# A fused attention, Fourier-mixing and feed-forward kernel: new constants for its list scheduler, and four pieces of work on other engines or queues

## The chip, the cores and the metric

The kernel runs on one core of one Trainium2 chip. The metric is the device time of one execution in microseconds (us). Before the change it is 1061.13 us, the median of three runs (1060.88 to 1061.39).

## What is computed

```python
# attention: q, k, v of 8 batches x 8 heads x 576 positions x 64
mask_plain = (rel >= 0) & (rel < 32)                    # heads 0 to 3
mask_dil   = (rel >= 0) & (rel < 128) & (rel % 4 == 0)  # heads 4 to 7
attn_out = softmax(where(mask, q @ k.T / 8, -1e9)) @ v
x = attn_out, heads side by side                        # (8, 576, 512)
mixed = real(fft(fft(x, axis=1), axis=2))
u  = x + mixed
un = (u - mean(u)) / sqrt(var(u) + 1e-6)                # over the 512 channels
out = u + relu(un @ w_ch1) @ w_ch2                      # 512 -> 2048 -> 512
```

The weights arrive as 64-bit floats, and the kernel turns them into 32-bit ones itself. Products that need full precision are done in three matmuls: each operand is split into a high and a low part (`hi*hi + lo*hi + hi*lo`).

## The kernel before, in words

The kernel is not written in the order in which it runs. A class `Plan` collects operations (`add`: engine, an estimated cost, what is read and written, a priority), and `Plan.run` then plays a list schedule: each engine that is free takes the available operation of lowest priority number whose buffers are free. The order so found is emitted once; on the chip each engine works through its own list in that order and waits on semaphores. Constants at the top of the file (`P_QK`, `P_MIX0`, `P_FILL` and so on) shift the priorities of kinds of work, others say how many buffers or units are treated in one way.

The work has two phases.

In the first phase (0 to 588 us of the trace) there are 96 **attention units**, 12 in each batch, six of dilated heads and six of plain ones; batch 0 begins with the dilated ones. A unit takes two blocks of 96 positions of two heads: eight score matmuls (L582), four masked copies with a running minimum on VectorE (L591), four exponentials on ScalarE (L597), four transposes (L610), a copy (L613), eight matmuls with v (L617), and on VectorE the division by the sums (L625 to L629) into a tile `xt`. Each pair of heads needs three loads, `tq`, `kb` and `vt` (L566 to L568), issued on SyncE's DMA queue (SP). The finished `xt` goes to DRAM from the same queue (`store`, L681). The plain heads of batch 0 go straight into the tiles `x` and `xtail` of the next step (`place`, L646, 11 DMAs).

After a batch's attention comes its **mix** (`mix`): three **folds** add and subtract mirrored rows (t1, t2 at L770 and L772, low parts at L792 and L794), matmuls along the sequence (L821, L843) and along the channels (L867, L873) follow with tables of cosines and sines, then `add_u` on GpSimd (POOL, L734 and L736), and `normalise`. Batch 0's tiles are transposed on TensorE (L715), those of the others come back from DRAM. The two tables are loaded from GpSimd's DMA queue by `tables_after`: `seq` after attention unit number NSEQ, `chn` after unit number NCHN.

Each pair of normalised tiles is a **fill** (`fill`): up-projection (L997) and down-projection (L1013) with the first six of 16 column blocks of the weights. Its weights are 12 tiles of 512 KB, each narrowed from 64 bits by four VectorE operations (L942 to L951) and split (`two_parts`: high part on ScalarE, L957; low part, L959, on POOL or, for the first NLW tiles, on VectorE).

In the second phase (from 588 us) the other ten blocks are applied to chunks of 512 tokens (L1277, L1369, L1336).

The eight PSUM banks are shared out by unit number. The scores of units below NSC2 use two pairs of banks in turn (`half2`), one of which is the pair `mix`; no `mix` bank is given out before the last of these units is done with it. The products with v of units below NAV2 use two banks in turn (`av2`), one of which belongs to `ff`; no fill gets an `ff` bank before the last of these is free. Until the first `ff` bank is given out, the planner puts **filler matmuls** on zeros (L515, two at a time, NSPIN tries) wherever TensorE has nothing else; from then on they vanish.

The change touches the constants, `dma` (L493), `place`, `normalise` and `fold`. What sets the first phase's order beside them are these lines:

```python
tables: if num == NSEQ: add("POOL", 0.3, ... tensor_copy(out=gone(), in_=xt()...))   # L537, L544
plan.behind.update({"av": ("av2",), "ff": ("av2",), "half": ("half2",), "mix": ("half2",)})
add("PE", 0.22, turn_over, (blank,), (spin,), SPIN, at=0.4 * n)                       # L515
```

Of the kernel before, what the change touches and what calls it, by code (L numbers as in the profile page):

```python
# [14 lines left out]
AF = mybir.ActivationFunctionType  # L15
ALU = mybir.AluOpType

B, H, S, D = 8, 8, 576, 64
C, FF = 512, 2048
P = 128  # L20
# [16 lines left out]
NPE = 1  # L37
LO1 = 'DVE'
NFA = 5
NSC2, NAV2 = 21, 32  # L40
NU0, NU1 = 9, 9
NFD, NUD, NLW = 1, 0, 0
P_QK0, P_V0 = -8, -7
P_ST, P_FD, P_WD, P_ST0, P_FD0, P_SPAN0, P_SPAN1 = -9.92, -2.8, -14.79, -21.37, -25.12, 7.59, 23.92
P_QK, P_V, P_TR, P_MIX, P_SPAN, P_W, P_WF, P_FILL, P_FILLT = -7.53, -11.06, -5.0, 3.7, 13.0, 27.01, 3.96, 47.55, 3.61
P_MIX0, P_MIX1 = -24.21, 7.67
NSEQ, NCHN = 4, 10
NCH = B * S // TOK
NREST = 4 * B
QB = 96  # L50
# [135 lines left out]
class Plan:  # L186
# [21 lines left out]
    def add(self, eng, cost, fn, r=(), w=(), prio=0.0, nbytes=0, at=0.0):  # L208
        op = Op()
        op.eng, op.cost, op.fn, op.prio, op.nbytes = eng, cost, fn, prio, nbytes  # L210
        op.num, op.after, op.ready, op.start = len(self.ops), [], at, None
        self.ops.append(op)
        deps, bufs = set(), {}
        for items, writes in ((r, False), (w, True)):
            for it in items:
                b, key = it if isinstance(it, tuple) else (it, None)
                bufs[id(b)] = b
                keys = set(b.writer) | set(b.readers) if key is None else {key, None}
                for x in keys:
                    if x in b.writer:  # L220
                        deps.add(b.writer[x])
                    if writes:
                        deps.update(b.readers.get(x, ()))
        for items, writes in ((r, False), (w, True)):
            for it in items:
                b, key = it if isinstance(it, tuple) else (it, None)
                if writes:
                    if key is None:
                        b.writer, b.readers = {None: op.num}, {}
                    else:  # L230
                        b.writer[key] = op.num
                        b.readers.pop(key, None)
                else:
                    b.readers.setdefault(key, []).append(op.num)
        op.bufs = list(bufs.values())
        for b in op.bufs:
            b.left += 1
        deps.discard(op.num)
        op.waits = len(deps)
        for d in deps:  # L240
            self.ops[d].after.append(op)
        return op
# [119 lines left out]
def act(n):  # L362
    return n * 0.00083 + 0.1
# [27 lines left out]
def fused_kernel(ctx: ExitStack, tc, q, k, v, w1, w2, seq, tail, chn, alt, mask, ident, perm, flip, out):  # L391
    nc = tc.nc
    plan = Plan()
    add = plan.add
# [50 lines left out]
    def work(tag, shape, dtype=F32, bufs=2):  # L445
        return plan.buf(lambda: pools["mix"], tag, shape, dtype, bufs)
# [46 lines left out]
    def dma(fn, r, w, prio, nbytes, slow=1):  # L493
        return add("SP", 0.5, fn, r, w, prio, nbytes * slow)

    def start():
# [139 lines left out]
    def place(u, val, xt, prio):  # L638
        tiles = (xs[0], xs[2], xtail[0]), (xs[1], xs[3], xtail[1])
        for n, (e, row, side, lo, rows) in enumerate((  # L640
# [3 lines left out]
        )[u]):  # L644
            x, p0 = tiles[e][row // P], row % P
            dma(lambda x=x, p0=p0, side=side, lo=lo, rows=rows: nc.sync.dma_start(  # L646
                out=x()[p0:p0 + rows, 0:C // 2], in_=val()[lo:lo + rows, side]),
                (xt,), ((x, ("plain", u, n)),), prio + P_ST0, rows * 1024)

# [42 lines left out]
    def normalise(u, idx, prio):  # L692
        stats, ve, r0, r1 = (work(t, [P, n]) for t, n in (("stats", 6), ("ve", 1), ("r0", 1), ("r1", 1)))
        uc = work("uc", [P, C + 2], F32, NUC)
        add("DVE", 0.6, lambda: nc.vector.bn_stats(out=stats(), in_=u()[:, 0:C]), ((u, 0),), (stats,), prio)
        add("DVE", 0.08, lambda: nc.vector.bn_aggr(out=uc()[:, C:C + 2], in_=stats()), (stats,), ((uc, 1),), prio)
        add("DVE", 0.4, lambda: nc.vector.tensor_scalar(
            uc()[:, 0:C], u()[:, 0:C], uc()[:, C:C + 1], None, op0=ALU.subtract), ((u, 0), (uc, 1)), ((uc, 0),), prio)
        add("DVE", 0.07, lambda: nc.vector.tensor_scalar(
            ve(), uc()[:, C + 1:C + 2], EPS, None, op0=ALU.add), ((uc, 1),), (ve,), prio + 1)  # L700
        add("POOL", 0.47, lambda: nc.gpsimd.tensor_tensor(
            out=r0(), in0=ve(), in1=half(), op=ALU.pow), (ve, half), (r0,), prio + 1)
        add("DVE", 0.07, lambda: nc.vector.tensor_scalar(
            r1(), ve(), r0(), r0(), op0=ALU.mult, op1=ALU.mult), (ve, r0), (r1,), prio + 1)
        add("DVE", 0.07, lambda: nc.vector.tensor_scalar(
            r1(), r1(), -0.5, 1.5, op0=ALU.mult, op1=ALU.add), (r1,), (r1,), prio + 1)
        add("DVE", 0.07, lambda: nc.vector.tensor_scalar(
            uc()[:, C + 1:C + 2], r1(), r0(), None, op0=ALU.mult), (r0, r1), ((uc, 2),), prio + 1)
        dma(lambda: nc.sync.dma_start(out=u_rows(idx), in_=uc()), (uc,), ((us[idx // 4], idx % 4),), prio + 1, P * 2056)
        return uc  # L710
# [28 lines left out]
    def mix(b, when):  # L739
# [10 lines left out]
        def fold(m, prio):  # L750
            early = prio + (P_FD if b else P_FD0)
            n = P if m < 2 else 33
            cs = slice(0 if b else C // 2, C)
            if m < 2:
                xp, xm = tiles[m]
                at = slice(0, P)
                for x, src in ((xp, plus), (xm, minus)):
                    dma(lambda x=x, src=src: nc.sync.dma_start(out=x()[:, cs], in_=src()[P * m:P * m + P, cs]),
                        (src,), ((x, 0),), early, P * (2048 if b else 1024))
            else:  # L760
                xp, xm = xtail
                at = slice(o, o + n)
                for x, key, src, lo, p0, k in (
                    (xp, 0, plus, 256, o, 32), (xm, 0, minus, 256, o, 32),
                    (xp, 1, minus, 288, o + 32, 1), (xm, 1, minus, 0, o + 32, 1),
                ):
                    dma(lambda x=x, src=src, lo=lo, p0=p0, k=k: nc.sync.dma_start(
                        out=x()[p0:p0 + k, cs], in_=src()[lo:lo + k, cs]), (src,), ((x, key),), early, k * 2048)
            t1, t2 = work("t1", [P, NEH], F32, 1), work("t2", [P, NEH], F32, 1)
            either(b < NFD, NEH, lambda on: on.tensor_tensor(  # L770
                out=t1()[at], in0=xp()[at, 0:NEH], in1=xm()[at, C:C // 2 - 1:-1], op=ALU.add), (xp, xm), (t1,), prio)
# [688 lines left out]
```

## Time and profile before

| what | value |
|---|---|
| median of 3 runs | 1061.13 us |
| the profiled execution's own time | 1064.29 us |
| its span, first to last instruction | 1062.5 us |
| TensorE busy | 1053.0 us of the span |
| VectorE, ScalarE, GpSimd busy | 775.7, 516.5, 272.8 us |
| mean granted TensorE clock | 0.998 of full speed |

Busy time is read from the recorded start and end of each instruction; consecutive matmuls overlap, so a stretch in which TensorE is always busy may still hold short waits. PE is TensorE, PEld its weight loads, DVE is VectorE, ACT ScalarE, POOL GpSimd, SP SyncE. A DMA queue's issuing instructions are listed under SPq or POOL.

### The profile page before, as it was taken

To read this page: it belongs to the slowest core of one execution; us is meant where nothing else is said; L and a number is where in the kernel's file an instruction comes from. 1 tells how busy PE (TensorE), PEld (TensorE's weight loads), DVE (VectorE), ACT (ScalarE), POOL (GpSimd) and SP (SyncE) were. 2 spreads that over 40 slices of the span, in tenths; PEclk is the share of its full clock that TensorE was granted. 3 is DMA by queue.
4 is the path that set the end of the run, shared out by engine and by line. 5 is a ranking of instruction groups with operands and counts; after the bars stand their busy time and mean duration, and the time that the engine had idled before them with its cause. 6 is when DMAs were issued, how large, how long until landed. Compare 5 with 4: busy or idle time off the path is not lost.

```text
span 1062.5 us, 21052 instructions
## 1 busy us (share of the span) xinstructions
PE 1053.0 (99%) x7641; PEld 950.7 (89%) x7641; DVE 775.7 (73%) x2398; ACT 516.5 (49%) x1282; POOL 272.8 (26%) x318
## 2 busy tenths in 40 slices
PE   9999999999999999999999999999999999999998
PEld 8898989889888989998999899999999999999987
DVE  6798987878775866786777566767676767575845
ACT  7767855564654653533443543525252525252522
POOL 1234354536541633563321110101010101010200
PEclk9999999999999999999999999999999999999999
DMA  9778656466454425335263212332233233232211
GB/s 345 214 239 261 185 183 197 135 188 196 149 177 136 130 66 172 108 111 156 95 197 110 90 40 51 110 71 91 74 99 84 81 93 78 87 77 84 80 61 40
DMA packets 103902, 136.51 MB, mean 128 GB/s; under 512 B 9247, under 2 KB 62496, under 8 KB 103798
## 3 DMA queue, kind: packets, MB, share of 16 engines
q1 hardware_dynamic: 100230, 126.26, 39.3%
q0 software_dynamic: 3040, 8.09, 2.6%
q8 instruction: 60, 0.98, 0.4%
q10 hardware_dynamic: 528, 0.82, 0.2%
q14 instruction: 44, 0.36, 0.1%
HBM read 97.33 MB, written 37.21 MB: 127 GB/s over the span
## 4 chain that ended last, share of the span: by engine, by line
PE 93%; DVE 3%; DMA 2%; ACT 1%; SPq 1%; issue 0%; DVEq 0%
PE bank L1277 23%; PE bank L1369 20%; PE bank L997 13%; PE bank L1013 13%; PE bank L617 6%; PE bank L582 5%; PE bank L867 3%; PE bank L821 3%; PE bank L610 3%; PE bank L515 2%; PE bank L1336 1%; DMA xsm<-xt 1%; PE bank L843 1%; DMA wst<-in_w_dram 1%; ACT pm L597 0%; DVE low L1005 0%
## 5 line engine op out<-in xcount | busy, mean ns | idle before, releaser
L1277 PE MATMUL bank<-low,wb 128*128 128x512 f32 x1080 | 257.0, 390 | 0.0
L1277 PEld LDWEIGHTS bank<-low,wb 128*128 128x128 f32 x1080 | 198.2, 188 | 38.2
L997 PE MATMUL bank<-ut,low 128*128 128x256 f32 x1296 | 169.4, 284 | 0.3 <-DVE low L1005 0.3
L997 PEld LDWEIGHTS bank<-ut,low 128*128 128x128 f32 x1296 | 158.8, 189 | 3.3 <-DVE low L1005 0.9
L1013 PE MATMUL bank<-low 128*128 128x512 f32 x648 | 155.1, 392 | 0.1
L597 ACT ACTIVATE pm<-pm,mx 96x128 f32<-96x128 f32 x384 | 128.3, 393 | 42.1 <-DVE mx L591 37.6
L1041 POOL DMA_INDIRECT ut<-us,flip_sb x20 | 40.5, 2023 | 402.4 <-DVE ut L1098 246.8
L1013 PEld LDWEIGHTS bank<-low 128*128 128x128 f32 x648 | 118.9, 188 | 23.4 <-DVE low L1005 0.3
L1283 ACT ACTIVATE xa<-bank 128x256 f32<-128x256 f32 x90 | 34.4, 382 | 176.9 <-PE bank L1277 176.9
L591 DVE CUSTOM_DVE_ANT_0 pm<-bank,mask_sb 96x128 f32<-96x128 f32 x384 | 92.3, 279 | 25.7 <-PE bank L582 23.2
L1308 DVE TENSOR_TENSOR y<-xa 128x384 f32<-128x384 f32 x45 | 25.1, 557 | 104.4 <-ACT xa L1283 104.2
L617 PE MATMUL bank<-vt,ptsb 128*96 128x65 f32 x768 | 80.8, 247 | 2.4 <-DVE xt L629 2.2
L617 PEld LDWEIGHTS bank<-vt,ptsb 128*96 128x96 f32 x768 | 75.6, 164 | 7.2 <-DVE xt L629 2.9
L1120 DVE STREAM_TRANSPOSE ut<-ut 128x512 f32<-128x512 f32 (+1 forms) x76 | 71.4, 981 | 11.6 <-DMA ut<-us 11.6
L1003 ACT ACTIVATE low<-bank 128x256 fp32r<-128x256 f32 x108 | 41.4, 384 | 76.3 <-PE bank L997 75.8
L1005 DVE SCALAR_TENSOR_TENSOR low<-bank,low 128x256 fp32r<-128x256 f32 x108 | 45.2, 420 | 41.2 <-ACT low L1003 40.8
L1369 PEld LDWEIGHTS bank<-w2s,low 128*128 128x128 f32 x588 | 73.2, 189 | 2.1
L1087 DVE TENSOR_TENSOR ut<-ut,bank 128x512 f32<-128x512 f32 (+1 forms) x136 | 73.1, 547 | 2.2
L1369 PE MATMUL bank<-w2s,low 128*128 128x256 f32 x588 | 73.8, 281 | 0.0
L582 PE MATMUL bank<-kb,tq 64*96 64x128 f32 x768 | 63.5, 288 | 0.2
L1369 PEld LDWEIGHTS bank<-w2s,hm 128*128 128x128 f32 x483 | 60.1, 188 | 1.8
L1369 PE MATMUL bank<-w2s,hm 128*128 128x256 f32 x483 | 60.6, 279 | 0.0
(159 smaller groups left out, 1794.1 us busy)
## 6 DMA issues: line engine op xcount, KB each, us to landing
vt<-in_v_dram SPq DMA_DIRECT2D x32, 390.0 KB
us<-uc SPq DMA_DIRECT2D x36, 257.0 KB
tq<-in_q_dram SPq DMA_DIRECT2D x32, 288.0 KB
part<-row SPq DMA_DIRECT2D x36, 256.0 KB
wst<-in_w_dram SPq DMA_DIRECT2D x18, 512.0 KB
ut<-us SPq DMA_DIRECT2D x36, 256.0 KB
ut<-part SPq DMA_DIRECT2D x36, 256.0 KB
kb<-in_k_dram SPq DMA_DIRECT2D x31, 288.0 KB
```

What stands on the lines that cost most here:

```text
L582: nc.tensor.matmul(sc()[e][:QB, KB * n:KB * n + KB], lhsT=tq()[ps, QB * t:QB * t + QB], rhs=kb()[ps, QB * t:QB * t + KB], start=True, stop ...
L591: nc.vector.tensor_tensor_reduce(pm()[:, i], sc()[i % 2][:QB, KB * (i // 2):KB * (i // 2) + KB], mask_sb()[:, masks[blocks[i // 2]]], -0.1 ...
L597: add("ACT", 0.295, lambda i=i: nc.scalar.activation(out=pm()[:, i], in_=pm()[:, i], func=AF.Exp, bias=mx()[:, i:i + 1], scale=-1.0), ((mx ...
L617: add("PE", 0.173, lambda i=i: nc.tensor.matmul(av()[:QB, 65 * i:65 * i + 65], lhsT=pt()[:, i], rhs=vt()[:, i % 2, blocks[i // 2]], start= ...
L997: nc.tensor.matmul(z()[:, :n_tok], lhsT=wf()[:, a, kk], rhs=ut()[:, p, kk], start=(kk == 0 and n == 0), stop=(kk == KT - 1 and n == 2),)
L1003: add("ACT", act(n_tok) - 0.05, lambda: nc.scalar.activation(out=h()[:, 0, :n_tok], in_=z()[:, :n_tok], func=AF.Relu), (z,), ((h, 0),), prio)
L1005: add("DVE", dve(n_tok), lambda: nc.vector.scalar_tensor_tensor(h()[:, 1, :n_tok], z()[:, :n_tok], 0.0, h()[:, 0, :n_tok].bitcast(F32), op ...
L1013: nc.tensor.matmul(acc(), lhsT=h()[:, a, P * s:P * s + P], rhs=wf()[:, p], start=(first and n == 0), stop=(last and n == 2),)
L1087: add("DVE", dve(C if at in (outer, inner) else TOK1), lambda: nc.vector.tensor_tensor(out=blocks(part())[:, at], in0=blocks(part())[:, at ...
L1120: nc.vector.transpose(out=o[back], in_=x[:, g])
L1277: nc.tensor.matmul(z(), lhsT=wb1[NF1 + 2 * p + f]()[:, a, kk], rhs=ut()[:, x, kk], start=(kk == 0 and n == 0), stop=(kk == KT - 1 and n == 2),
L1369: nc.tensor.matmul(acc()[block // 2][:, TOK1 * (block % 2):TOK1 * (block % 2) + TOK1], lhsT=hl()[:, a, i], rhs=w2s[p]()[:, j, x], start=(o ...
```

## The change

The constants of the list schedule get new values: scores with two bank pairs for units below 25 instead of 21 (NSC2), products with v on two banks below unit 30 instead of 32 (NAV2), `seq` tables after unit 6 instead of 4 (NSEQ), `chn` tables after unit 14 instead of 10 (NCHN), one weight buffer claimed one tile later (NU1), and other priority shifts. Batch 0's four fold sums and differences (t1, t2 and the two low parts, in each of three folds) go from VectorE to GpSimd (NFD 1 to 0). The low parts of the first four weight tiles go from GpSimd to VectorE (NLW 0 to 4). The 11 DMAs of `place` are issued on GpSimd's queue instead of SyncE's (QD 2). The other new options are left off: QF 0 keeps batch 0's fold loads on SyncE's queue, SUB0 and SUB1 of 0 keep the subtraction of the mean on VectorE.

```diff
-NSC2, NAV2 = 21, 32
-NU0, NU1 = 9, 9
-NFD, NUD, NLW = 1, 0, 0
-P_QK0, P_V0 = -8, -7
-P_ST, P_FD, P_WD, P_ST0, P_FD0, P_SPAN0, P_SPAN1 = -9.92, -2.8, -14.79, -21.37, -25.12, 7.59, 23.92
-P_QK, P_V, P_TR, P_MIX, P_SPAN, P_W, P_WF, P_FILL, P_FILLT = -7.53, -11.06, -5.0, 3.7, 13.0, 27.01, 3.96, 47.55, 3.61
-P_MIX0, P_MIX1 = -24.21, 7.67
-NSEQ, NCHN = 4, 10
+NSC2, NAV2 = 25, 30
+NU0, NU1 = 9, 10
+NFD, NUD, NLW = 0, 0, 4
+P_QK0, P_V0 = -5.02, -5.15
+P_ST, P_FD, P_WD, P_ST0, P_FD0, P_SPAN0, P_SPAN1 = -19.19, -17.91, -17.11, -14.67, 5.44, 7.55, 15.79
+P_QK, P_V, P_TR, P_MIX, P_SPAN, P_W, P_WF, P_FILL, P_FILLT = -11.03, -7.38, -5.0, 4.77, 11.08, 27.01, 3.0, 57.63, 3.17
+P_MIX0, P_MIX1 = -14.83, 7.35
+NSEQ, NCHN = 6, 14
+QD, QF = 2, 0
+SUB0, SUB1 = 0, 0
...
+    def dma_on(way, fn, r, w, prio, nbytes):
+        eng, cost, q = (("SP", 0.5, nc.sync), ("ACT", 0.4, nc.scalar), ("POOL", 0.55, nc.gpsimd))[way]
+        return add(eng, cost, lambda: fn(q), r, w, prio, nbytes)
...
-            dma(lambda x=x, p0=p0, side=side, lo=lo, rows=rows: nc.sync.dma_start(
+            dma_on(QD, lambda q, x=x, p0=p0, side=side, lo=lo, rows=rows: q.dma_start(
                 out=x()[p0:p0 + rows, 0:C // 2], in_=val()[lo:lo + rows, side]),
                 (xt,), ((x, ("plain", u, n)),), prio + P_ST0, rows * 1024)
...
-                    dma(lambda x=x, src=src: nc.sync.dma_start(out=x()[:, cs], in_=src()[P * m:P * m + P, cs]),
-                        (src,), ((x, 0),), early, P * (2048 if b else 1024))
+                    dma_on(0 if b else QF, lambda q, x=x, src=src: q.dma_start(out=x()[:, cs], in_=src()[P * m:P * m + P, cs]),
+                           (src,), ((x, 0),), early, P * (2048 if b else 1024))
```

## Rows read from the trace of the kernel before

**Rows 1.** The page's busy us, share of the span and instructions.

```profile
PE 1053.0 (99%) x7641; PEld 950.7 (89%) x7641; DVE 775.7 (73%) x2398; ACT 516.5 (49%) x1282; POOL 272.8 (26%) x318
```

**Rows 2.** Windows of all engines: us, busy (x instructions) by engine, clock, DMA share, GB/s.

```profile
7.00:30.00 23.00, 22.02 (x239) 19.31 (x239) 17.10 (x115) 19.77 (x58) 4.30 (x7) 1.00 1.03 364
30.00:48.00 18.00, 17.10 (x167) 15.17 (x169) 15.65 (x96) 14.16 (x41) 5.36 (x8) 0.91 0.67 196
48.00:61.00 13.00, 13.00 (x126) 12.69 (x124) 11.08 (x44) 7.32 (x21) 1.26 (x1) 1.00 0.95 290
...
78.00:94.00 16.00, 15.92 (x167) 14.38 (x166) 13.71 (x88) 10.35 (x31) 7.37 (x11) 1.00 0.86 265
94.00:108.00 14.00, 13.94 (x140) 12.38 (x139) 13.23 (x81) 12.63 (x38) 6.46 (x8) 1.00 0.66 213
108.00:150.00 42.00, 41.51 (x396) 37.72 (x395) 38.38 (x188) 32.15 (x89) 20.14 (x22) 1.00 0.59 180
```

**Rows 3.** The same windows, the filler matmuls of line 515 alone (PE, PEld, clock, DMA).

```profile
7.00:30.00 23.00, 6.26 (x34) 4.59 (x34) 1.00 1.03 364
30.00:48.00 18.00, 5.56 (x28) 4.15 (x28) 0.91 0.67 196
48.00:61.00 13.00, 7.89 (x54) 6.81 (x54) 1.00 0.95 290
...
78.00:94.00 16.00, 6.37 (x38) 5.09 (x38) 1.00 0.86 265
94.00:108.00 14.00, 4.34 (x28) 3.58 (x28) 1.00 0.66 213
```

**Rows 4.** Timeline of PE: start us, us, line, operation, count [idle before <-releaser].

```profile
23.29 0.68 PE L582 MATMUL bank<-kb,tq 64*96 64x128 f32 x8
23.90 0.74 PE L515 MATMUL bank<-blank 128*128 128x256 f32 x4
...
25.56 0.68 PE L582 MATMUL bank<-kb,tq 64*96 64x128 f32 x8
...
30.90 1.07 PE L617 MATMUL bank<-vt,ptsb 128*96 128x65 f32 x8 [1.87 <-DVE xt L629]
...
48.69 2.87 PE L515 MATMUL bank<-blank 128*128 128x256 f32 x22
...
60.76 0.68 PE L582 MATMUL bank<-kb,tq 64*96 64x128 f32 x8
...
83.76 0.75 PE L715 MATMUL bank<-ident_sb,uc 128*128 128x128 f32 x4
...
93.65 0.89 PE L617 MATMUL bank<-vt,ptsb 128*96 128x65 f32 x8
...
98.99 0.86 PE L617 MATMUL bank<-vt,ptsb 128*96 128x65 f32 x8
...
107.82 1.28 PE L997 MATMUL bank<-ut,low 128*128 128x256 f32 x9
```

**Rows 5.** Timeline of SP's DMA queue, the plain stores (L646) and what follows.

```profile
41.50 2.51 SPq L646 DMA_DIRECT2D x<-xt  x4
...
55.56 0.46 SPq L566 DMA_DIRECT2D kb<-in_k_dram  x1
```

**Rows 6.** Timeline of POOL: the tables, a weight low part.

```profile
15.89 1.30 POOL L533 DMA_DIRECT2D seq<-in_seq_dram  x2
...
38.57 1.27 POOL L959 TENSOR_TENSOR low<-ut,low 128x512 fp32r<-128x512 f32 x1 [9.32 <-ACT low L957]
```

**Rows 7.** One line's instructions, L770: duration ns min/median/max, first and last start.

```profile
L770 POOL TENSOR_TENSOR t<-x,x x14: 727/736/1121, 95.3 to 420.4; 128x257 f32<-128x257 f32 x14
...
L770 DVE TENSOR_TENSOR t<-x,x x2: 416/423/430, 53.7 to 55.5; 128x257 f32<-128x257 f32 x2
```

**Rows 8.** The same view of L948.

```profile
L948 DVE SCALAR_TENSOR_TENSOR ut<-ut x14: 671/682/1491, 22.7 to 584.4; 128x512 uint32<-128x512 uint32 x14
```

**Rows 9.** The same view of L1140.

```profile
L1140 DVE TENSOR_TENSOR low<-ut,low x36: 680/683/692, 580.8 to 987.7; 128x512 fp32r<-128x512 f32 x36
```

More of the change, by code (lines that the diff above doesn't have):

```diff
@@ L696, in normalise @@
         add("DVE", 0.08, lambda: nc.vector.bn_aggr(out=uc()[:, C:C + 2], in_=stats()), (stats,), ((uc, 1),), prio)
-        add("DVE", 0.4, lambda: nc.vector.tensor_scalar(
-            uc()[:, 0:C], u()[:, 0:C], uc()[:, C:C + 1], None, op0=ALU.subtract), ((u, 0), (uc, 1)), ((uc, 0),), prio)
+        if SUB0 if idx < 4 else SUB1:
+            less = work("less", [P, 1])
+            add("DVE", 0.07, lambda: nc.vector.tensor_scalar(
+                less(), uc()[:, C:C + 1], -1.0, None, op0=ALU.mult), ((uc, 1),), (less,), prio)
+            add("ACT", act(C), lambda: nc.scalar.activation(
+                out=uc()[:, 0:C], in_=u()[:, 0:C], func=AF.Identity, bias=less(), scale=1.0), ((u, 0), less), ((uc, 0),), prio)
+        else:
+            add("DVE", 0.4, lambda: nc.vector.tensor_scalar(
+                uc()[:, 0:C], u()[:, 0:C], uc()[:, C:C + 1], None, op0=ALU.subtract), ((u, 0), (uc, 1)), ((uc, 0),), prio)
         add("DVE", 0.07, lambda: nc.vector.tensor_scalar(
@@ L766, in fold @@
                 ):
-                    dma(lambda x=x, src=src, lo=lo, p0=p0, k=k: nc.sync.dma_start(
+                    dma_on(0 if b else QF, lambda q, x=x, src=src, lo=lo, p0=p0, k=k: q.dma_start(
                         out=x()[p0:p0 + k, cs], in_=src()[lo:lo + k, cs]), (src,), ((x, key),), early, k * 2048)
```

## The prediction

> **What bounds the kernel now.** The page's busy line comes first: TensorE is busy for 1053.0 of 1062.5 us, and no other engine for more than 775.7 [rows 1]. Only 9.5 us of the span are idle, so waits as the profile lists them hold almost nothing to win. The question is what TensorE is busy with. The view of line 515 alone answers it: from 7 to 108 us it runs 182 matmuls on zeros (34 + 28 + 54, none from 61 to 78, 38 + 28) [rows 3]. They are the plan's own idle time made visible. The reader is to see in the PE timeline what one costs: 22 of them start at 48.69 us and take 2.87 us including the last one's tail of about 0.17 us (a matmul's record is longer than the step to the next), so (2.87 - 0.17) / 22 = 0.12 us each, and 182 of them 22 us [rows 4]. A change of order can win this, and waits; everything else TensorE does is the same work in either kernel.
>
> Next, what keeps TensorE short of work before 108 us. In steady flow an attention unit follows the last after 25.56 - 23.29 = 2.27 us, and about 0.58 us of that is fillers (four of them begin at 23.90 us), so a unit is 1.7 us of TensorE work [rows 4]. The windows show the others near their limits at different times: DMA at 1.03 from 7 to 30 us and 0.95 from 48 to 61, VectorE at 11.08 of 13 us from 48 to 61 and 13.23 of 14 from 94 to 108 [rows 2]. Three places stand out in the PE timeline. At 30.90 us TensorE resumes after 1.87 us of idling for a VectorE division into `xt` [rows 4]; in the window from 30 to 48 us the granted clock averages 0.91, which is 3.2 us at the lower of its two levels (1.2 of 2.4 GHz), worth 1.6 us [rows 2]. From 48.69 to 60.76 us no unit starts its scores and 54 fillers run [rows 3, 4]. And at 107.82 us the first fill begins; after that there are no fillers, and the 42 us to 150 us are 41.51 busy [rows 2, 4]. So the first fill's start is the switch, and the time until then is what the change acts on.
>
> **Part by part.** The sums are made against the profiled execution, 1064.29 us by its own time, 1.8 us more than its span; that is 3.2 us above the median of the runs shown, and I take the same 3.2 us off at the end.
>
> *Tables later (NSEQ 4 to 6, NCHN 10 to 14).* The `seq` tables are issued from 15.89 us, inside the window in which DMA is full [rows 2, 6]. Two units later is 4.5 us later by the 2.27 us step [rows 4], so q, k, v and the stores of `xt` go first. What may go is the 1.87 us stall and the 1.6 us of low clock behind it, 3.5 us together. The same bytes still have to move, and the next `xt` buffer may be late instead, so the bounds are 0 and 3.5 us; I take 2.
>
> *Plain stores on GpSimd's queue (QD 2).* SP issues these 11 DMAs from 41.50 us, the first four in 2.51 us, each behind an `xt`; what waits behind them on SP are the loads of batch 1, whose `kb` of 55.56 us is among those that the units after the gap need [rows 5]. Off SP, the loads can go some 7 us earlier (11 x 0.63 us). On GpSimd an issue takes 1.30 / 2 = 0.65 us [rows 6], so 11 cost 7.2 us there. Queued behind the waiting ones are GpSimd's weight low parts, the `chn` tables and batch 0's folds, which need those stores anyway. GpSimd is busy 5.36 of 18 and 1.26 of 13 us here, so there is room [rows 2].
>
> *Fold sums on GpSimd, four low parts on VectorE.* Three folds times four operations leave VectorE at 0.42 us each, 5.0 us, and cost GpSimd 0.74 us each, 8.8 us [rows 7]. Four low parts leave GpSimd at 1.27 us, 5.1 us [rows 6], and cost VectorE at most 0.68 us each, the row of the same shape, 2.7 us [rows 9]. VectorE gains 2.3 us net, but in the window that matters the folds' 5.0 us are nearly all of what it lacked. The fold chain gets 12 x 0.32 = 3.8 us longer.
>
> There is a row against this move: L948 takes 1.491 us at worst against a median of 0.682 [rows 8], beside a GpSimd low part of 38.57 us [rows 6]; GpSimd work can hold up VectorE. It is a rare row, so I charge 1 us for it. The Trainium skill (SBUF — State Buffer, "Who interferes with whom") makes it a rule: a VectorE instruction with two inputs in SBUF and a GpSimd instruction that reads SBUF exclude each other, and the second waits for the whole of the first. By that rule the worst case would be 12 hits of 0.81 us, 9.7 us of VectorE, and the move would lose what it gained; this trace agrees with the rule in kind, since 0.81 us is about two thirds of a low part's 1.27.
>
> *Two bank pairs for four more units (NSC2 21 to 25).* Units 21 to 24 are those that would fill the gap from 48.69 to 60.76 us: four units are 6.8 us of TensorE work, the 54 fillers 6.5 us. VectorE has 1.9 us free in that window plus the 5.0 us of folds, which is 6.9 us, or four units at about 1.6 us (four masked copies, the sums and the division). DMA at 0.95 is what speaks against it [rows 2, 3]. Bounds 0 and 6.5 us; I take half, 3.2.
>
> The price is that mix 0 gets its banks four units later, 9.1 us, on top of the fold's 3.8. Its first pair is transposed at 83.76 us and first used at 107.82, so there are 23 us of cover [rows 4]; 12.9 us fit in.
>
> *Fills from unit 30 (NAV2 32 to 30).* The first fill waits for the last unit that uses the shared bank. Counting the L617 groups of eight, that was unit 31 at 98.99 us and would be unit 29 at 93.65 [rows 4]: 5.3 us earlier. At 28 fillers in the last 14 us (3.4 us, 0.24 us per us) that is 1.3 us. Bounds 0 and 3.4.
>
> *Other constants.* Fill, weight and mix priorities reorder work in a stretch where TensorE is full already; I put new short waits at 1.5 us of loss, between 2 of gain and 5 of loss (the 0.49 us that TensorE misses between 108 and 150 us, carried over the 480 us to the second phase, is 5.6) [rows 2]. The second phase has the same instructions in the same order, so nothing.
>
> Sum: 2 + 3.2 + 1.3 - 1.5 = 5.0 us, the 1 us for VectorE's hold-ups being inside the halved 3.2. 1064.3 - 5.0 = 1059.3 us profiled, and less 3.2 a median of 1056 us.
>
> **The rivals.**
>
> *DMA is the bound.* From 7 to 30 us it is full and moves 364 GB/s, from 48 to 61 it is at 0.95 [rows 2]. If loads land no sooner, the fillers only move: fewer in the last window, more before. Only the gate (1.3) is left, against 1.5 of new waits: 1061 us. Against it speaks the 0.67 from 30 to 48 us.
>
> *Mix 0 becomes the gate, and the kernel gets slower.* If the first pair of tiles is transposed after unit 29 is done, each us beyond costs fillers at 0.24 to 0.5 us per us (28 x 0.12 in 14 us, 54 x 0.12 in 13). The cover of 23 us less 5.3 for the earlier gate is 18; bank and fold take 12.9. It decides from 5 us more: GpSimd's queue with 7.2 us of issues, 8.8 of sums and the `chn` tables four units (9 us) later can give that and, with all of it in series, 20 us more than the cover. The first fill then starts 15 to 20 us late by the gate, for 15 x 0.24 to 20 x 0.5, 4 to 10 us; with the waits 1.5, and with the gain of the tables gone, about 1067 us. For it: all new GpSimd work lies in this one chain. Against it: mix 0 has its cover.
>
> *Everything closes.* The stall, its clock, the gap and the gate at their upper bounds: 3.5 + 6.5 + 3.4 = 13.4 us, 1048 us.
>
> **How the numbers follow.** Forecast 0.45, its own range 1052 to 1059; DMA 0.20; mix 0 as gate 0.20; everything 0.15. The range from 1047 to 1067 leaves out about 1 in 10 above and less below. What tells a gain from none is 0.2%, 2.1 us. Faster: the forecast nearly whole, 0.42, everything 0.15, and some of the DMA case, 0.03, makes 0.60. Same: 0.17, most of the DMA case and a little of the forecast. Slower: 0.23, mix 0 and the rest.
>
> **What would show it.** Fillers from 7 us on: about 140 instead of 182 if I am right, over 182 in the slower case. First L997 near 95 to 102 us instead of 107.82; no stall of over 1 us on `xt` near 30 us and a granted clock near 1.00 from 30 to 48 us. Scores of units 21 to 24 inside what was the gap. The last L715 of the first pair before unit 29's L617: if not, mix 0 is the gate. A window from 150 us to the second phase that loses more than 2 us against the old one, or a second phase of another length, would prove the reasoning about the rest wrong.

## The result, and the profile after

The changed kernel takes 1070.06 us (median of 7, 1066.71 to 1072.91), the kernel before 1061.41 in the same runs: a ratio of 1.008, interval 1.0069 to 1.0091. It is 8.7 us slower where 5 us faster was forecast, and outside the range that was given. The profiled execution of the changed kernel took 1068.77 us.

Two things went the way that was forecast. Fillers fell from 206 to 182 in all (from 7 us on, as the prediction counts them, from 182 to about 153), and the first fill moved forward. The second phase, from the first L1290 on (L1277 before), is as long as it was: 474.3 us, 474.6 before. The page's busy line first, as for [rows 1]:

```profile
PE 1052.6 (99%) x7617; PEld 948.3 (89%) x7617; DVE 776.1 (73%) x2390; ACT 516.0 (48%) x1282; POOL 287.6 (27%) x337
```

Then the windows that answer to [rows 2], the whole span of the first fill and the stretch behind it:

```profile
7.00:30.00 23.00, 21.20 (x231) 18.48 (x230) 17.61 (x117) 18.84 (x56) 0.96 (x3) 1.00 0.85 293
30.00:48.00 18.00, 17.27 (x182) 14.96 (x179) 15.49 (x95) 14.37 (x41) 8.56 (x16) 1.00 1.05 337
48.00:61.00 13.00, 13.00 (x140) 12.01 (x140) 11.78 (x67) 11.67 (x36) 6.80 (x12) 1.00 1.09 348
61.00:78.00 17.00, 14.21 (x118) 12.41 (x118) 12.05 (x52) 11.60 (x33) 7.47 (x7) 0.90 0.52 184
78.00:94.00 16.00, 16.00 (x156) 15.38 (x155) 14.41 (x67) 8.92 (x23) 13.19 (x16) 1.00 0.55 165
94.00:108.00 14.00, 13.94 (x140) 12.63 (x138) 12.20 (x75) 9.37 (x27) 6.97 (x11) 1.00 0.86 268
108.00:150.00 42.00, 41.95 (x395) 37.24 (x392) 38.38 (x183) 31.33 (x87) 23.22 (x28) 1.00 0.59 182
```

The fillers alone (L521 in this kernel), as in [rows 3]:

```profile
48.00:61.00 13.00, 5.33 (x34) 4.39 (x34) 1.00 1.09 348
...
78.00:94.00 16.00, 5.76 (x33) 4.48 (x34) 1.00 0.55 165
94.00:108.00 14.00, 3.51 (x24) 2.91 (x23) 1.00 0.86 268
```

From 48 to 61 us there are 34 fillers instead of 54. But DMA is now full from 30 to 61 us (1.05 and 1.09, where it was 0.67 and 0.95) and has room at the start (0.85, where it was 1.03), and from 61 to 78 us TensorE, which was busy throughout before, loses 2.79 us and runs at a granted clock of 0.90. That window before:

```profile
61.00:78.00 17.00, 17.00 (x169) 15.34 (x167) 15.96 (x71) 12.96 (x35) 6.82 (x8) 1.00 0.62 213
```

The PE timeline (start us, us, line, count, idle before), as in [rows 4]:

```profile
9.86 1.12 PE L588 MATMUL bank<-kb,tq 64*96 64x128 f32 x16 [1.80 <-DMA tq<-in_q_dram]
...
64.32 2.30 PE L834 MATMUL bank<-seq,ees 128*128 128x290 f32 x8 [2.54 <-POOL ees L805]
...
93.37 0.68 PE L728 MATMUL bank<-ident_sb,uc 128*128 128x128 f32 x4
...
95.88 0.89 PE L623 MATMUL bank<-vt,ptsb 128*96 128x65 f32 x8
...
101.86 0.95 PE L1010 MATMUL bank<-ut,low 128*128 128x256 f32 x6
```

The first scores start at 9.86 us after 1.80 us of waiting for `tq` (before, they started at 6.86 us, in the row below). The first sequence matmuls (L834) stop for 2.54 us until a low part of a fold, on GpSimd, is there; behind that stop lies the low clock, 0.10 of 17 us, 1.7 us. The first pair of tiles is transposed by 94 us, unit 29 is at 95.88, and the first fill starts at 101.86 us, 6.0 earlier than in [rows 4]. The gate moved as the prediction said; the time was lost elsewhere. The first scores before:

```profile
6.86 1.45 PE L582 MATMUL bank<-kb,tq 64*96 64x128 f32 x16
```

Where the time was lost is seen in GpSimd's timeline. `gone` is the small copy that releases a table:

```profile
29.04 0.18 POOL L543 COPY gone<-xt 1x1 f32<-1x1 f32 x1 [28.60 <-DVE xt L635]
...
44.65 0.75 POOL L783 TENSOR_TENSOR t<-x,x 128x257 f32<-128x257 f32 x1
53.26 0.17 POOL L550 COPY gone<-xt 1x1 f32<-1x1 f32 x1 [7.86 <-DVE xt L635]
53.40 0.72 POOL L785 TENSOR_TENSOR t<-x,x 128x257 f32<-128x257 f32 x1
...
55.74 1.07 POOL L539 DMA_DIRECT2D chn<-in_chn_dram  x2
56.82 0.74 POOL L783 TENSOR_TENSOR t<-x,x 128x257 f32<-128x257 f32 x1
...
61.69 2.58 POOL L805 TENSOR_TENSOR ees<-ee,ees 128x257 fp32r<-128x257 f32 x1
```

Fold 0's first sum (L783) runs at 44.65 us. The next instruction in GpSimd's queue is the copy that releases the channel tables; it waits 7.86 us for attention unit 14's `xt`. Behind it stand the second sum (L785), the tables' five DMAs, issued until 56.81 us, and fold 1's first sum (the second L783). At 61.69 us a low part (L805), which takes 0.74 us in the median, takes 2.58: the one that TensorE waits for. VectorE's timeline beside it:

```profile
54.38 0.41 DVE L797 TENSOR_TENSOR ee<-t,t 128x257 f32<-128x257 f32 x1
54.72 0.41 DVE L799 TENSOR_TENSOR oo<-t,t 128x256 f32<-128x256 f32 x1
...
61.82 0.68 DVE L958 SCALAR_TENSOR_TENSOR ut<-ut 128x512 uint32<-128x512 uint32 x1
...
63.10 0.68 DVE L961 SCALAR_TENSOR_TENSOR ut<-ut 128x512 uint32<-128x512 uint32 x1
```

The second sum is not too late for its reader: it ends at 54.12 us, and VectorE comes to it (L797) at 54.38, with no idle time before. What is late is fold 1's first sum: VectorE is done with fold 0's (L799) at 55.13 us, and the sum starts 1.69 us after that, behind the tables' DMAs. Later, three weight-narrowing steps (L958, L955, L961) and a division follow each other without a gap until 63.78 us, and GpSimd's low part ends 0.49 us later. That GpSimd waits for VectorE here is read from the overlap; no run isolates it.

**Before, once more.** Run f1 is the kernel before, unchanged: 1061.15 us, and this execution took 1061.30, where the profiled one ahead of the prediction took 1064.29. Three rows of it:

```profile
30.00:48.00 18.00, 18.00 (x191) 16.16 (x191) 17.35 (x105) 16.75 (x51) 5.36 (x8) 1.00 0.87 239
```

```profile
29.59 0.89 PE L617 MATMUL bank<-vt,ptsb 128*96 128x65 f32 x8 [0.88 <-DVE xt L629]
...
104.99 1.28 PE L997 MATMUL bank<-ut,low 128*128 128x256 f32 x9
```

The granted clock from 30 to 48 us is 1.00 instead of 0.91, and the stall is 0.88 instead of 1.87 us. The 3.5 us that the prediction hoped to win near 30 us [rows 2, 4] were for the most part that one execution's. So were 2.8 of the 6.0 us by which the first fill came earlier: here it starts at 104.99 us, 3.1 later than in the changed kernel.

### The profile page after: what moved, and what is told of

It reads as the page before. It is cut to its first block, busy times and chain, and to the rows that moved or that the text cites. A ratio compares the mean times of both kernels' runs of the same rounds, so it can differ in the third digit from the quotient of the medians.

```text
span 1067.0 us, 21051 instructions
## 1 busy us (share of the span) xinstructions
PE 1052.6 (99%) x7617; PEld 948.3 (89%) x7617; DVE 776.1 (73%) x2390; ACT 516.0 (48%) x1282; POOL 287.6 (27%) x337
## 4 chain that ended last, share of the span: by engine, by line
PE 91%; DMA 3%; DVE 3%; POOL 1%; issue 1%; ACT 0%; SPq 0%; DVEq 0%; POOLq 0%; ACTq 0%
PE bank L1290 23%; PE bank L1382 20%; PE bank L1026 13%; PE bank L1010 13%; PE bank L623 5%; PE bank L588 5%; PE bank L834 3%; PE bank L880 3%; PE bank L616 3%; PE bank L1349 1%; PE bank L521 1%; DMA seq<-in_seq_dram 1%; DVE pm L597 1%; PE bank L856 1%; DMA ut<-us 1%
## 5 line engine op out<-in xcount | busy, mean ns | idle before, releaser
L1290 PE MATMUL bank<-low,wb 128*128 128x512 f32 x1080 | 257.0, 390 | 0.0
L1290 PEld LDWEIGHTS bank<-low,wb 128*128 128x128 f32 x1080 | 198.2, 188 | 38.2
L623 PE MATMUL bank<-vt,ptsb 128*96 128x65 f32 x768 | 80.6, 248 | 0.7 <-DVE xt L635 0.4
L623 PEld LDWEIGHTS bank<-vt,ptsb 128*96 128x96 f32 x768 | 74.2, 164 | 5.8 <-DVE xt L635 1.0
```

The costliest lines, as they stand in the source:

```text
L623: add("PE", 0.173, lambda i=i: nc.tensor.matmul(av()[:QB, 65 * i:65 * i + 65], lhsT=pt()[:, i], rhs=vt()[:, i % 2, blocks[i // 2]], start= ...
L1290: nc.tensor.matmul(z(), lhsT=wb1[NF1 + 2 * p + f]()[:, a, kk], rhs=ut()[:, x, kk], start=(kk == 0 and n == 0), stop=(kk == KT - 1 and n == 2),
```

## The experiments

Since one changed constant makes the planner write another order, most experiments keep the plan and change only what is emitted: an operand, an engine or a queue, with every engine's list otherwise in its old order. Runs e7, e8, f2, f3 and f4 are planned anew. Times are medians; ratios are to the kernel before, with 95% intervals. The changed kernel itself is at 1.008 (1.0069 to 1.0091).

| run | base | what is different | us | ratio (interval) |
|---|---|---|---|---|
| e1 | after | channel trigger freed | 1065.64 | 1.0043 (1.0029 to 1.0058) |
| e2 | after | first loads as before | 1070.09 | 1.0079 (1.0053 to 1.0105) |
| e3 | after | fold sums on VectorE | 1067.50 | 1.0049 (1.0030 to 1.0068) |
| e4 | after | plain stores on SP | 1072.84 | 1.0101 (1.0080 to 1.0122) |
| e5 | after | both triggers freed | 1064.13 | 1.0051 (1.0021 to 1.0081) |
| e6 | after | both triggers, first loads | 1063.81 | 1.0027 (1.0006 to 1.0047) |
| e7 | before | all moves, planned anew | 1080.32 | 1.0180 (1.0158 to 1.0203) |
| e8 | after | constants only, planned anew | 1065.92 | 1.0040 (1.0024 to 1.0056) |
| e9 | before | fold sums on GpSimd | 1062.05 | 1.0008 (0.9995 to 1.0020) |
| e10 | before | plain stores on GpSimd | 1062.67 | 1.0015 (1.0004 to 1.0025) |
| e11 | before | four low parts on VectorE | 1062.74 | 1.0011 (1.0000 to 1.0023) |
| e12 | before | first loads as after | 1063.82 | 1.0017 (1.0005 to 1.0029) |
| f1 | before | nothing | 1061.15 | 0.9995 (0.9984 to 1.0007) |
| f2 | before | later constants of after | 1067.82 | 1.0056 (1.0040 to 1.0071) |
| f3 | before | early constants of after | 1076.08 | 1.0153 (1.0130 to 1.0176) |
| f4 | after | both triggers, later constants of before | 1069.90 | 1.0072 (1.0055 to 1.0089) |

**e1: the channel trigger freed.** Its copy reads a constant instead of `xt`.

```diff
         if num == NCHN:
-            add("POOL", 0.3, lambda: nc.gpsimd.tensor_copy(out=gone(), in_=xt()[0:1, 0, 0, 0:1]), ...
+            add("POOL", 0.3, lambda: nc.gpsimd.tensor_copy(out=gone(), in_=half()[0:1]), ...
```

> The changed kernel with one operand replaced: the small copy on GpSimd that releases the channel tables reads a constant instead of attention unit 14's output. Every engine keeps its order; only the wait is gone that holds GpSimd's queue for 7.86 us between the first and the second sum of fold 0. Theory A (mix 0's chain of sums on GpSimd costs the time): the first sequence matmul no longer waits 2.5 us, the window from 61 to 78 us has a granted clock near 1.00 instead of 0.90, and the time falls by about 4 us, from 1070 to 1066. Theory B (the first loads of q and k stand behind the constants) and theory C (many small waits spread from 150 to 590 us): within 1 us of the changed kernel.

It is 4.4 us faster than the changed kernel, and the intervals lie apart. GpSimd's timeline:

```profile
44.91 0.17 POOL L550 COPY gone<-half 1x1 f32<-1x1 f32 x1
49.42 0.86 POOL L785 TENSOR_TENSOR t<-x,x 128x257 f32<-128x257 f32 x1 [4.34 <-DMA x<-xt]
...
56.88 0.92 POOL L783 TENSOR_TENSOR t<-x,x 128x257 f32<-128x257 f32 x1 [3.90 <-issue]
...
61.92 0.63 POOL L805 TENSOR_TENSOR ees<-ee,ees 128x257 fp32r<-128x257 f32 x1
```

VectorE's:

```profile
56.32 0.41 DVE L799 TENSOR_TENSOR oo<-t,t 128x256 f32<-128x256 f32 x1
...
62.05 1.75 DVE L958 SCALAR_TENSOR_TENSOR ut<-ut 128x512 uint32<-128x512 uint32 x1
```

The copy no longer waits. The second sum does, 4.34 us, for a plain store that lands late; still it starts 4.0 us earlier than in the changed kernel. That lead goes no further in this profile: fold 1's first sum starts at 56.88 us, where it started at 56.82. But it now follows VectorE's L799 by 0.15 us instead of 1.69, since the tables' DMAs are out by 52.97 us. The low part, at 61.92 us, takes 0.63 us, and TensorE does not wait for it; now it is VectorE's step beside it (L958) that takes 1.75 us instead of 0.68. The profiles fall into two groups by this: e2 and e4, which keep the trigger, have the changed kernel's pair (low part 2.58, L958 0.68 or 0.69), e5 and e6, which free it, have that of e1 (0.63 and 1.74). The window from 61 to 78 us, against 14.21 busy at clock 0.90:

```profile
48.00:61.00 13.00, 13.00 (x127) 11.88 (x126) 10.97 (x64) 11.05 (x34) 6.54 (x10) 0.87 1.11 365
61.00:78.00 17.00, 16.86 (x156) 15.24 (x155) 16.45 (x64) 13.03 (x36) 6.33 (x8) 1.00 0.61 205
```

The 2.65 us of busy time are back there, and the clock; a low clock of 0.87 has come from 48 to 61 us instead, after a wait of the scores at 46 us. So the times show that the late trigger costs about half of the loss. By the profiles it does so through TensorE's stop and the clock behind it; the stop hangs on which of the two engines is held up, and how the trigger decides that is not shown. That the tables themselves land earlier is not the gain: in the changed kernel their last DMA is issued by 56.81 us and lands within 6.5 us, and they are first used at 76.11 us (L880).

**e2: the first loads.** The first eight of SP's DMAs are put back in the order of the kernel before.

```diff
-        for o in order:
+        for o in swapped(order):    # SP's first eight: tq, mask, ident, perm, vt, kb, tq, vt
```

> The changed kernel with the first eight DMAs of SP's queue in the order of the kernel before (first tq, then mask, identity and permutation tables, vt, kb, tq, vt). All else keeps its order, the 29 planned fillers ahead of the first scores too. Theory B: the 1.8 us wait of the first scores for tq goes, first scores near 8.1 us instead of 9.9, time lower by about 1.8 us, 1068. Theories A and C: the wait goes as well but is taken up by what comes later (the fold sums on GpSimd, or the many waits): within 0.7 us of the changed kernel.

```profile
8.12 1.12 PE L588 MATMUL bank<-kb,tq 64*96 64x128 f32 x16
```

The first scores start 1.74 us earlier, and the time does not move. The wait behind the trigger does not take up all of that: TensorE's stop, 2.56 us here, ends at 63.01 us instead of 64.32, so 1.3 us are left. They go in the low clock behind it:

```profile
61.00:78.00 17.00, 14.99 (x116) 13.09 (x116) 11.12 (x43) 10.59 (x29) 6.13 (x6) 0.80 0.45 158
```

0.20 of 17 us are 3.4 us, where the changed kernel lost 1.7, and the first fill starts at 101.57 us, 0.3 earlier. That is one execution; theory B alone does not explain the loss. Run **e12** does the reverse on the kernel before (the order mask, ident, perm, vt, tq, vt, kb, tq):

```diff
-        for o in order:
+        for o in swapped(order):    # SP's first eight: mask, ident, perm, vt, tq, vt, kb, tq
```

> The kernel before in its own order, with the first DMAs of SP's queue in the order of the changed kernel (mask, identity and permutation tables and vt ahead of the first tq). Theory B: the first scores come 2 to 3 us later than 6.9 us and nothing takes it up, 1063 to 1064. If later waits take it up, as in the run that put them back: within 0.7 us of before.

There the first loads cost 1.8 us by the ratio (0.5 to 3.1), a little less than B said. In its profile the first scores start at 9.28 us after 3.00 us of waiting for `tq`, and the granted clock from 7 to 30 us is 0.85.

**e3: fold sums on VectorE**, at the places that the plan gave them.

```diff
-        on = nc.vector if dve_ else nc.gpsimd
+        on = nc.vector if dve_ or here else nc.gpsimd    # here: batch 0's t1, t2 and low parts
```

> The changed kernel with batch 0's twelve fold sums and differences emitted on VectorE instead of GpSimd, each at the place that the plan gave it; all else keeps its order. Theory A: VectorE takes 5.0 us more, but no sum stands behind the table trigger and none of 2.58 us is held up by the shared work of the two engines; the first sequence matmul does not wait, and the time is 2 to 4 us lower, 1066 to 1068. Theory C: no gain, 0 to 3 us slower, since VectorE is the fuller engine there.

2.6 us faster than the changed kernel by the medians, intervals just apart (1.0068 against 1.0069). Taken out of GpSimd's queue, the sums neither stand behind the trigger nor run beside VectorE's steps; e3 does not tell the two apart. **e9** is the opposite edit on the kernel before, whose trigger is done before the folds begin:

```diff
-        on = nc.vector if dve_ else nc.gpsimd
+        on = nc.vector if dve_ and not here else nc.gpsimd
```

> The kernel before in its own order, with batch 0's twelve fold sums and differences emitted on GpSimd at the places the plan gave them on VectorE. Theory A (a longer fold chain on GpSimd costs): the first sequence matmul at 57.5 us waits for the sums, 2 to 5 us slower, 1063 to 1066. The prediction's step (VectorE wins 5.0 us where it is short, the chain has cover): within 1 us of before.

No difference that can be told: the longer chain has its cover there, as the prediction said. The sums on GpSimd show a cost only behind that trigger.

**e4: plain stores back on SP**, and **e10: plain stores on GpSimd** in the kernel before.

```diff
-            dma_on(QD, lambda q, ...: q.dma_start(
+            dma_on(QD, lambda q, ...: nc.sync.dma_start(       # e4
...
-            dma(lambda ...: nc.sync.dma_start(
+            dma(lambda ...: nc.gpsimd.dma_start(               # e10
```

> The changed kernel with the 11 plain stores of batch 0 emitted on SP's queue instead of GpSimd's, each at the place that the plan gave it. Theory A: the stores themselves do no harm on GpSimd, since it has room until 44 us; back on SP they hold up loads of batch 1, so 0 to 3 us slower than the changed kernel (1070 to 1073). If the stores on GpSimd's queue are what costs the time, it is 2 us or more faster (1068 or less).

> The kernel before in its own order, with the 11 plain stores emitted on GpSimd's queue, which leaves SP free from 41.5 to 49 us. The prediction's step: loads of batch 1 go earlier, but TensorE's order is fixed with its fillers in it, so 0 to 2 us faster, 1059 to 1061. Theory A: GpSimd's low part at 51 us and the channel tables stand among these stores and come later, 0 to 2 us slower.

e4's interval overlaps that of the changed kernel, and its profile has the same stop (2.54 us); the stores on GpSimd's queue are not what made it slow. On the kernel before they cost 1.6 us by the ratio (0.4 to 2.7), not the gain of 0 to 2 us that I expected. That a plan whose fillers are written in can't use an earlier load is likely, and not shown.

**e5: both triggers freed.** The copy that releases the sequence tables is put after unit 1 and reads unit 1's `xt`.

```diff
-            add("POOL", 0.3, lambda: nc.gpsimd.tensor_copy(out=gone(), in_=xt()[0:1, 0, 0, 0:1]), ...
+            add("POOL", 0.3, lambda: nc.gpsimd.tensor_copy(out=gone(), in_=EARLY[1][1]()[0:1, 0, 0, 0:1]), ...
...
-        for o in order:
+        for o in earlier(order):    # the copy and its five loads after unit 1's division
```

> The changed kernel with both table triggers freed: the channel tables' copy reads a constant (as in the run before), and the copy that releases the sequence tables stands after unit 1 and reads unit 1's output, so that it fires near 18 us instead of 29, as it did at 15.7 us in the kernel before. Every engine keeps its order. Theory D (the late sequence tables fill the DMA engines from 30 to 61 us, so the plain stores land late, the next xt buffer is late, VectorE and TensorE wait): the 1.3 us wait of scores near 46 us and the low clock from 48 to 61 us go, the time is 2 to 3 us below the kernel with the channel trigger alone (1065.6), near 1063. Against it: the tables take their 5 us of DMA time from q, k and v earlier instead, and the time stays within 1 us of 1065.6.

```profile
7.00:30.00 23.00, 20.64 (x225) 17.74 (x223) 16.46 (x111) 18.27 (x54) 3.19 (x6) 1.00 1.02 357
30.00:48.00 18.00, 17.55 (x183) 15.46 (x184) 17.56 (x103) 15.62 (x45) 9.18 (x16) 1.00 0.92 284
48.00:61.00 13.00, 13.00 (x139) 12.01 (x138) 12.07 (x72) 12.17 (x37) 6.60 (x11) 1.00 1.11 359
61.00:78.00 17.00, 16.85 (x155) 15.24 (x155) 16.41 (x63) 12.59 (x35) 6.56 (x8) 1.00 0.53 179
```

The DMA share is as before again (1.02, then 0.92), the granted clock is 1.00 throughout, and the median is 1.5 us below e1; but the ratio is above that of e1, since three of the twelve executions took over 1071 us, and the interval (1.0021 to 1.0081) is wide and holds that of e1. So this gain is not shown by the times. **e6** is e5 with e2's `swapped(order)` around the same list:

> The same as the run with both triggers freed, and the first eight DMAs of SP's queue in the order of the kernel before as well. Theory B together with D: once nothing in mix 0's chain waits, the 1.8 us that the first scores win are kept, 1 to 2 us below the run with both triggers freed (1061 to 1062). If the first loads are hidden anyway: within 0.7 us of it.

0.3 us below e5, no difference. Against the changed kernel e6 is 6.2 us faster, intervals far apart (at most 1.0047 against at least 1.0069), and 0.6 to 5.0 us slower than before.

**The clock of each execution.** Every execution also has a mean granted clock over its span. In f1 it is 0.999 or 1.000 in nine of ten executions; of the changed kernel in none of seven (0.991 to 0.998, 0.995 on average). The 0.005 that are missing are 5 us of 1068, where f1 misses 0.7 on average. By this estimate, which takes it that TensorE sets the pace wherever its clock is low, about half of the 8.7 us is low clock, more than the 1.7 us that the one profile shows. And among executions at 0.999 or more, e1 (4 of 12, 1062.9 to 1065.5 us), e5 (8 of 12, 1061.8 to 1064.4) and e6 (9 of 12, 1061.8 to 1064.2) can't be told apart: what the second trigger gives, if anything, is a clock that falls less often, and these counts are too small to show it.

**e11: four low parts on VectorE** in the kernel before.

```diff
-        lo = nc.gpsimd if eng == "POOL" else nc.vector
+        lo = nc.gpsimd if eng == "POOL" and not any(key[0] is x for x in wa1[:2] + wa2[:2]) else nc.vector
```

> The kernel before in its own order, with the low parts of the first four weight tiles emitted on VectorE. All theories: VectorE takes 2.7 us more between 28 and 52 us, where it waits anyway; within 1 us of before (1060 to 1062).

0 to 2.4 us slower; the medians differ by 1.75, a little more than the 1 us I had allowed.

**e7: the moves without the constants, and e8: the constants without the moves**, both planned anew.

```diff
+NFD, NUD, NLW = 0, 0, 4        # e7: with NSEQ, NCHN = 6, 14 and QD = 2; every other constant of before
...
+NFD, NUD, NLW = 1, 0, 0        # e8: with NSEQ, NCHN = 4, 10 and QD = 0; every other constant of after
```

> The kernel before with its own priorities and bank limits, and the moves alone: plain stores on GpSimd's queue, batch 0's fold sums on GpSimd, four low parts on VectorE, tables after units 6 and 14; planned anew. Theory A (the moves put mix 0's chain behind waits on GpSimd's queue): 3 us or more slower than before, 1064 to 1070. Theory C (the new priorities cost the time): within 2 us of before, 1059 to 1063.

> The kernel after with its new priorities and bank limits, but the moves undone: plain stores on SP, fold sums on VectorE, low parts on GpSimd, tables after units 4 and 10; planned anew. Theory C (the new priorities cost the time, by small waits from 150 us on): 3 us or more slower than before, 1064 to 1070. Theory A (the moves cost it): within 2 us of before, 1059 to 1063. Both together, some 3 to 5 us slower, if each part has its share.

The moves alone cost 19 us, more than twice the whole change; the constants alone 4.5. The new constants took back more than half of what the moves cost. e7's GpSimd and PE rows:

```profile
54.16 0.17 POOL L550 COPY gone<-xt 1x1 f32<-1x1 f32 x1 [9.71 <-DVE xt L635]
```

```profile
47.03 0.89 PE L623 MATMUL bank<-vt,ptsb 128*96 128x65 f32 x8 [3.02 <-DVE xt L635]
...
116.50 0.62 PE L1010 MATMUL bank<-ut,low 128*128 128x256 f32 x3
```

The channel trigger waits 9.71 us, the products with v (L623) 3.02 us for an `xt`, and the first fill starts at 116.50 us, behind 226 fillers. A late first fill and over 182 fillers are what the rival with mix 0 as the gate forecast; but the first pair of tiles is transposed by 93.5 us, ahead of unit 31's products, which end at 109.5, so by the prediction's own sign mix 0 is not the gate here. What holds the fill until 116.50 us is not shown.

**f1 to f4: which constants?** f2 and f3 set one half each on the kernel before, f4 takes the later half back on the changed kernel with both triggers freed.

```diff
+P_QK, P_V, P_TR, P_MIX, P_SPAN, P_W, P_WF, P_FILL, P_FILLT = -11.03, -7.38, -5.0, 4.77, 11.08, 27.01, 3.0, 57.63, 3.17   # f2
+P_ST, P_FD, P_WD, ..., P_SPAN1 = -19.19, -17.91, -17.11, ..., 15.79; P_MIX1 = 7.35                                        # f2
...
+NSC2, NAV2 = 25, 30; NU1 = 10; P_QK0, P_V0 = -5.02, -5.15; P_MIX0 = -14.83                                                # f3
+P_ST0, P_FD0, P_SPAN0 = -14.67, 5.44, 7.55                                                                                # f3
```

> The kernel before, unchanged, for a second profile of it (the first one's execution was 3.2 us above its median). All theories: 1061 us; its windows show how far the 9.5 us of idle time and the 0.91 granted clock from 30 to 48 us are its own and how far they were that execution's. If the stall near 30 us and the low clock are absent here, the span is near 1059 us.

> The kernel before with only those new priorities that act after batch 0 and 1's first work (stores, loads, fills, weights, mixes of the later batches); bank limits, first loads and the moves as before; planned anew. Theory C1 (the later priorities bring the small waits of 150 to 450 us): 3 to 5 us slower, 1064 to 1066, the windows from 150 to 450 us losing 2 to 4 us against before. Theory C2 (the early ones do): within 1.5 us of before.

> The kernel before with only the new constants that act early (two bank pairs up to unit 25, two banks for v up to unit 30, the first loads, batch 0's store, fold and mix priorities); planned anew. Theory C2: 3 to 5 us slower. Theory C1: within 1.5 us of before, or faster by up to 3 us by the fillers saved (before: 206).

> The changed kernel with both table triggers freed and the later priorities of the kernel before; early constants and moves as changed; planned anew. Theory C1: the rest of the loss goes with the later priorities, 1058 to 1061, faster than the run with the triggers freed alone (1064.1). Theory C2: 1063 to 1066.

Both theories fall. By the ratios f2 is 5.9 us over before, f3 16.2, and both halves together in e8 4.2: f3 alone is far slower than the two, f2 at least not better (its interval overlaps that of e8). Taking the later half back does not make e5 faster (f4's interval overlaps that of e5, its median is 5.8 us above, and its mean clocks go down to 0.989). The constants belong to one plan; a part of them is another plan, not a part of the change. Why f3 is that slow its profile tells in part: scores wait 5.4 us for the maxima,

```profile
PE bank L582 <- DVE mx L591: 5.4, 10, 2.3
```

and the stretch behind the first fill is short of work:

```profile
108.00:150.00 42.00, 40.38 (x386) 36.10 (x385) 37.20 (x187) 33.31 (x95) 13.16 (x14) 1.00 0.52 165
```

**What is left.** e6 leaves 0.6 to 5.0 us. Idle time of TensorE from 150 us on shows where most of that may lie. The kernel before (f1):

```profile
200.00:250.00 50.00, 49.97 (x439) 44.51 (x438) 40.54 (x206) 32.27 (x90) 25.40 (x37) 1.00 0.66 190
...
400.00:450.00 50.00, 50.00 (x331) 45.51 (x330) 33.85 (x69) 21.15 (x47) 22.74 (x26) 1.00 0.44 131
450.00:500.00 50.00, 48.78 (x317) 44.07 (x316) 40.38 (x86) 17.87 (x38) 23.27 (x26) 1.00 0.43 126
```

The same windows of the changed kernel:

```profile
200.00:250.00 50.00, 49.42 (x409) 43.39 (x408) 41.05 (x187) 27.49 (x78) 23.69 (x34) 1.00 0.58 175
...
400.00:450.00 50.00, 48.31 (x324) 43.63 (x324) 40.45 (x84) 21.01 (x48) 33.20 (x36) 1.00 0.37 113
450.00:500.00 50.00, 50.00 (x328) 45.68 (x327) 33.43 (x72) 15.74 (x33) 19.87 (x21) 1.00 0.41 127
```

Over the nine windows from 150 to 585 us (eight of 50 and one of 35 us), f1 is idle for 435 - 433.73 = 1.27 us, the changed kernel for 435 - 431.61 = 3.39 us (GpSimd is busy 33.20 us from 400 to 450 where it was 22.74). The ends of matmuls are modelled in the trace, so short waits may not show in it. e5 has the same order there and 3.50 us. That this is due to the priorities is plausible and not shown: f2 idles for 3.66 us there and is 6 us slower, but with other waits ahead of 150 us too. It stays open.

Nor do the parts add up. Between the two profiled executions, 1068.77 and 1061.30 us (f1), the stop of 2.5 us, the clock behind it of 1.7, the first loads' wait of 1.8 and the 2.1 us of later idle time, less 2.9 us of fillers, make 5.2 of 7.5 us. The rest is not located.

## Why the prediction was wrong

**Fewer fillers and an earlier fill: right, and smaller.** 24 fillers of 0.12 us are 2.9 us, where 42 and 5 were forecast. NAV2 did its part: the first fill came 6.0 us earlier (3.1 against f1), within the 95 to 102 us that were named. NSC2 closed part of the gap (54 fillers to 34).

**Tables later: the step that failed.** The prediction put the tables "two units later", 4.5 us by the unit's step, and their price at a gain of 2. The trigger row, 15.89 us [rows 6], contradicts that reading: at 2.27 us a unit, unit 4 can't be done by then. The copy reads a single element, which the first of two units that share a tile writes. With NSEQ 4 it waited for unit 1; with NSEQ 6 it waits for unit 6 itself, at 29.04 us, and with NCHN 14 for unit 14 itself, at 53.26. The real move is 13.3 us for the sequence tables, and the channel trigger became a wait of 7.86 us. What the prediction put in its sum as a gain of 2 us cost 4.4 us (e1); whether the sequence trigger adds to that is not shown (e5).

**Work moved to GpSimd: the second half of the same step.** I named what is queued behind the stores, the `chn` tables and the folds among it, and then called GpSimd's busy share "room". A queue in order has no room behind an instruction that waits. The sums by themselves are harmless (e9), the stores nearly so (e10: 1.6 us); sums and DMAs behind a trigger cost 2.6 to 4.4 us (e3, e1). The hold-up by the other engine, priced at 1 us on VectorE's side, came on GpSimd's: 2.58 instead of 0.74 us for the very sum that TensorE needed. With the trigger freed it is on VectorE's side (1.75 instead of 0.68 us, e1), and TensorE does not stop. The Trainium skill (SBUF — State Buffer, "Who interferes with whom") has both sides, the later one to issue being blocked. The traces agree in that both occur; they do not show the rule of the order, since by its record the low part starts 0.13 us ahead of VectorE's L958 in both cases (61.69 and 61.82 us, 61.92 and 62.05), and its 1.84 us are lost behind several VectorE instructions in a row.

**The first loads: overlooked.** P_QK0 from -8 to -5.02 moves q and k behind the constants' loads at -7.9 to -7; I put it under "other constants". In the kernel before this costs 1.8 us (e12); in the changed one the old order wins nothing that can be told, with the trigger in place (e2) or with both triggers freed (e6 against e5).

**The stall near 30 us: a term from one execution.** 1.87 us and a clock of 0.91 were 0.88 us and 1.00 in the next profile (f1). The profiled run's 3.2 us above the median should have been the warning: the sum took the stall and the clock off as the gain of 2, and once more within the 3.2 us that it subtracts at the end.

**Other constants: near the forecast.** The sum has 1.5 us of new waits; from 150 to 585 us the changed kernel idles 2.1 us more than f1. That is just over the 2 us that the prediction named as a sign against its reasoning on the rest.

**The rivals.** Mix 0's chain on GpSimd with the `chn` trigger in it was named as the slower case, at 1067 us with a chance of 0.20. Place and sign were right, the mechanism was not: its price was worked out by a later first fill, and that came earlier, with mix 0 off the gate (the first pair of tiles by 94 us, unit 29 at 95.88). TensorE paid directly: 2.54 us at the sequence matmuls and 1.7 us of clock.

## What to carry to other kernels

Before a wait is moved, look up in the trace what releases it now, and check that against the time at which the code's reading could be true; a dependency on one element can be a different one than the name says. On an engine that works in order, a trigger for a load is a wait for all that stands behind it, and the engine's idle share says nothing about that. Look at the granted clock of every execution before a microsecond or two is put down to an edit. Search constants of a list schedule are one point: take one edit at a time with the order held fixed, because half of such a set told nothing about the whole.

## What the runs showed of the hardware

A stop of TensorE of 2.54 us lies in a window of 17 us whose granted clock is 0.90 in the mean, between the levels of 1.2 and 2.4 GHz (e1 without the stop: 1.00 there): 0.10 of 17 us are 1.7 us, two thirds of the stop again. Low stretches in other profiles stand behind a stop too: 0.91 over 18 us behind 1.87 us (before), 0.87 over 13 us behind 1.30 us (e1), 0.85 over 23 us behind 3.00 us (e12). But not every stop brings one: behind 1.80 us at 9.86 us (the changed kernel), 2.10 us at 9.42 us (e5) and 2.27 us at 30.13 us (f3) the clock stays at 1.00, so the length of a stop does not tell whether it will. A GpSimd sum and a VectorE step that run beside each other: one of them took 1.1 or 1.8 us longer, GpSimd's in the changed kernel (2.58 instead of 0.74 us) and VectorE's in e1 (1.75 instead of 0.68).
